# Issuing the first weight load of a decode kernel ahead of the opening barrier

## The chip, the cores and the metric

The kernel runs on one core of one Trainium2 chip. The metric is the device time of one execution in microseconds; each run also has the span, from the start of the program's first instruction to the end of its last. A load is issued by an instruction, its data then come in packets, and it lands when all have arrived.

## The reference

A decode step: the gated sum of an attention block over a cached K and V and of a small dense block.

```python
# x: 2 x 1 x 448, wq: 448 x 4096, k_cache, v_cache: 2 x 8 x 32768 x 256, wo: 4096 x 448, all bf16
g = sigmoid((x * gate_w).sum(-1, keepdims=True))
q = (x @ wq).reshape(B, 1, 16, 256).transpose(0, 2, 1, 3)
p = softmax(einsum("bhqd,bhkd->bhqk", q, repeat(k_cache)) * 256 ** -0.5)
a = einsum("bhqk,bhkd->bhqd", p, repeat(v_cache)).transpose(...).reshape(...) @ wo
b = gelu(x @ w1 + b1) @ w2 + b2           # w1: 448 x 1792, w2: 1792 x 448
out = g * a + (1 - g) * b
```

The two caches are 537 MB of the 547 MB that must be read. Everything else is small.

## The kernel before

SyncE issues all large loads, in one order: WQ (two parts), W1 (two parts), then K and V tiles of 8 MB in turn, and W2 and WO at the end. The tiles go round three slots of on-chip memory. A load is issued when the work that read its slot has ended. ScalarE's queue brings six small loads: x, the gate (two rows), the biases b1 and b2 (three loads).

```python
def prog_sp(E):
    def dma(fn, stream, key):
        E.ins(fn, key=key, stream=stream)

    for d in order:
        for pd in before_of[d]:
            E.wait("pe", released(pd))          # wait until the slot is free
        kind, idx = d
        if kind == "WQ":
            parts = [(wq_f, A_wq[0:KC * P, :].rearrange("(p k) n -> p (k n)", p=P), "d_wq0"),   # 3 MB
                     (wq_r, A_wq[KC * P:Dm, :].rearrange("p (h n) -> (p h) n", h=2), "d_wq1")]  # 0.5 MB
            for i, (o, src, _) in enumerate(parts):
                dma(lambda e, o=o, src=src: e.dma_start(o, src), "slot0", ("wq", i))
        elif kind == "W1":
            ...                                  # 1.3 MB and 0.2 MB
        ...
        else:
            src = kv_src(A_k_cache if kind == "K" else A_v_cache, idx)
            dma(lambda e, src=src, d=d: e.dma_start(cut(slot_of[d], 0, SLOT), src),
                f"slot{slot_of[d]}", ("fill", d))
    ...

def prog_act(E):
    dma(lambda e: e.dma_start(x_sb, A_x[:, 0, :]), "d_x", "x")
    ...                                          # gate, b1, b2: five more small loads
```

The programs of the five engines start in a block. Ahead of it the framework puts an opening block: GpSimd writes four constants, every engine drains and reports to GpSimd, and GpSimd releases them all. This is the opening barrier.

```python
with nc.Block("main") as block:
    def run(nm, eng):
        engs[nm].eng = eng
        progs[nm](engs[nm])

    block.gpsimd(lambda eng: run("pool", eng))
    block.sync(lambda eng: run("sp", eng))
    ...
```

Of the kernel before, what the change touches and what calls it, by code (L numbers as in the profile page):

```python
# [125 lines left out]
def bass_gated_mix__gqa_block_cached__dense_activation_gelu__decode_kernel(  # L126
# [27 lines left out]
    _, Hkv, Sk, Dh = A_k_cache.shape  # L154
# [4 lines left out]
    P = 128  # L159
# [11 lines left out]
    KC = 3  # L171
# [29 lines left out]
    with contextlib.ExitStack() as es:  # L201
# [65 lines left out]
        def kv_src(cache, idx):  # L267
            g, t = idx // NT, idx % NT
            b, kvh = grp(g)
            return cache[b, kvh, t * P * R:(t + 1) * P * R, :].rearrange("(p r) d -> p (r d)", p=P)  # L270
# [32 lines left out]
        def released(d):  # L303
            kind, idx = d
            return {"K": ("S", idx, NCK // 2 - 1), "V": ("PV", idx), "WQ": "QT", "W1": "HT"}[kind]

        cut = lambda s, lo, n: ring[:, s * SLOT + lo:s * SLOT + lo + n]
        wq_f, wq_r = cut(0, 0, KC * HD), cut(0, KC * HD, HW)
# [31 lines left out]
        def prog_pool(E):  # L340
# [13 lines left out]
            for b in range(Bn):  # L354
                E.ins(lambda e, b=b: e.affine_select(
                    out=tsel[:, 136 * b:136 * b + 136], in_=tsel[:, 136 * b:136 * b + 136], compare_op=ALU.not_equal,
                    fill=1.0, base=256 - 128 * b, pattern=[[-1, 136]], channel_multiplier=-8), key=f"ts{b}")

        def prog_sp(E):
            def dma(fn, stream, key):  # L360
                E.ins(fn, key=key, stream=stream)

            for d in order:
                for pd in before_of[d]:
                    E.wait("pe", released(pd))
                kind, idx = d
                if kind == "WQ":
                    parts = [(wq_f, A_wq[0:KC * P, :].rearrange("(p k) n -> p (k n)", p=P), "d_wq0"),
                             (wq_r, A_wq[KC * P:Dm, :].rearrange("p (h n) -> (p h) n", h=2), "d_wq1")]
                    for i, (o, src, _) in enumerate(parts):  # L370
                        dma(lambda e, o=o, src=src: e.dma_start(o, src), "slot0", ("wq", i))
                elif kind == "W1":
                    parts = [(w1_f, B_w1[0:KC * P, :].rearrange("(p k) n -> p (k n)", p=P)),
                             (w1_r, B_w1[KC * P:Dm, :].rearrange("p (h n) -> (p h) n", h=2))]
                    for i, (o, src) in enumerate(parts):
                        dma(lambda e, o=o, src=src: e.dma_start(o, src), "d_w1", ("w1", i))  # L376
                elif kind == "W2":
                    dma(lambda e: e.dma_start(w2_f, B_w2.rearrange("(p f) n -> p (f n)", p=P)), "d_w2", "w2")
                elif kind == "WO":
                    src = A_wo.rearrange("(p c) n -> p (c n)", p=P)  # L380
                    for i in range(len(WOP) - 1):
                        c0, c1 = WOP[i] * Dm, WOP[i + 1] * Dm
                        dma(lambda e, src=src, c0=c0, c1=c1: e.dma_start(wo_v[:, c0:c1], src[:, c0:c1]), f"pW{i}", ("wo", i))  # L383
                elif d == ("V", LASTV):
                    src, base, r0 = kv_src(A_v_cache, idx), slot_of[d] * SLOT, 0
                    for i, n in enumerate(PIECES):
                        c0, c1 = r0 * Dh, (r0 + n) * Dh
                        dma(lambda e, c0=c0, c1=c1: e.dma_start(ring[:, base + c0:base + c1], src[:, c0:c1]),
                            f"pV{i}", ("piece", i))
                        r0 += n  # L390
# [4 lines that stand above are left out]
            E.wait_total("mix")  # L395
            dma(lambda e: e.dma_start(out[:, 0, :], out_sb), "d_out", "out")
            E.wait_total("d_out")
# [260 lines left out]
        def prog_dve(E):  # L658
# [134 lines left out]
            E.ins(lambda e: e.tensor_copy(out_sb[:, 0:DQ], ps_a[0:Bn, :]), key="mixd", stream="mix")  # L793

        progs = {"pool": prog_pool, "sp": prog_sp, "pe": prog_pe, "act": prog_act, "dve": prog_dve}
        engs = {nm: _Eng(sch, nm) for nm in progs}
        sch.plan = True
        for nm, f in progs.items():
            f(engs[nm])
        for stream, key in sch.reqs:  # L800
            assert key in sch.streams[stream].events, f"missing event {stream}:{key}"
        sch.plan = False
        sch.reset_counts()
        with nc.Block("main") as block:
            def run(nm, eng):
                engs[nm].eng = eng
# [4 lines that stand above are left out]
            block.tensor(lambda eng: run("pe", eng))  # L811
            block.scalar(lambda eng: run("act", eng))
            block.vector(lambda eng: run("dve", eng))
# [28 lines left out]
```

## Time and profile before

| kernel before | |
|---|---|
| time, median of 6 runs | 1272.86 us (1272.69 to 1272.92) |
| span of the profiled run | 1270.7 us |
| bytes moved, mean rate | 547.61 MB, 431 GB/s |
| first WQ load issued | 0.74 us |
| first packets of the stream | 1.77 us |
| last WO piece that the end waits for landed | 1268.12 us |

The page of the kernel before, cut to the DMA. The second line is the busy share of the DMA engines in tenths, in 40 equal slices of the span; the queue line gives packets, MB and the share of 16 engines' span that their packets took.

```profile
span 1270.7 us, 8089 instructions
...
DMA  9999999999999999999999999999999999999998
...
DMA packets 11116, 547.61 MB, mean 431 GB/s; under 512 B 1368, under 2 KB 1632, under 8 KB 2144
...
q1 hardware_dynamic: 10948, 547.43, 99.7%
q8 instruction: 9, 0.15, 0.0%
```

The engines that move data are busy all the time. Two edges are left, and the first is visible in the timeline of the opening (start, duration, engine; "SPq" is SyncE's own queue of instructions):

```profile
0.24 0.10 POOL L827 MEMSET const-float32-0.0<- 128x1 f32 x1 [0.24 <-issue]
...
0.73 0.56 ACTq L602 DMA_DIRECT2D pexp<-in_A_x_dram  x1
0.73 0.20 POOL L341 MEMSET ident_b<- 128x128 bf16 x1 [0.29 <-POOLq L827]
0.74 0.88 SPq L371 DMA_DIRECT2D ring<-in_A_wq_dram  x2
...
1.67 1.11 SPq L376 DMA_DIRECT2D ring<-in_B_w_dram  x2
...
2.81 22.79 SPq L393 DMA_DIRECT2D ring<-in_A_k_cache_dram  x3
```

SyncE begins at 0.00 us, yet issues its first load at 0.74 us. The list of SyncE's waits names what it did in between; L827 is the barrier:

```profile
SPq L827 <- PEq L827: 0.7, 1, 0.7
```

When the data begin to move is shown by short windows of the same kernel. The last two columns are the DMA share and GB/s. A packet is counted whole in the window in which it starts, so the share can be above 1: only the first window with a large number matters.

```profile
core 0: us, PE busy (x) PEld busy (x) DVE busy (x) ACT busy (x) POOL busy (x), PEclk, DMA share, GB/s
1.60:1.75 0.15, 0.00 (x0) 0.00 (x0) 0.15 (x1) 0.00 (x0) 0.15 (x2) 1.00 0.06 12
1.75:1.90 0.15, 0.00 (x0) 0.00 (x0) 0.15 (x1) 0.00 (x0) 0.15 (x2) 1.00 5.54 1311
```

The stream starts in the second window (the records have the first packet at 1.77 us), 1.03 us after the start of the issue, or 0.62 us after its end, since the first issue takes 0.41 us. Two lines of the chain of waits (start, duration, what) give the landing of the first K tile and of the fourth of WO's five pieces: 2.81 + 33.52 = 36.33 us and 1227.23 + 40.88 = 1268.11 us. The fifth piece, 0.9 KB a row, lands at 1268.38 us, while the matmuls on the fourth still follow each other without a break. So the fourth is the last piece that the end waits for; it is what the prediction and the text below call the last WO piece.

```profile
2.81 33.52 DMA ring<-in_A_k_cache_dram
...
1227.23 40.88 DMA ring<-in_A_wo_dram
```

### The profile page before, as it was taken

How to read it: one execution, taken by the hardware profiler on the slowest of the kernel's cores; microseconds unless marked ns; L12 is line 12 of the kernel's file. 1: busy time of each engine (PE TensorE's matmuls, PEld its weight loads, DVE VectorE, ACT ScalarE, POOL GpSimd, SP SyncE). 2: the span in 40 equal slices, each digit the busy share in tenths (PEclk: the TensorE clock that was granted, in tenths of full speed). 3: DMA queues.
4: the chain of work that ended last, by engine and by line, in shares of the span. 5: the costliest groups of instructions: out<-in, count | busy, mean ns of one | idle time of the engine just before them, and what ended most of it. 6: DMA issues, size and time to landing. Idle time of an engine off the chain costs nothing.

```text
span 1270.7 us, 8089 instructions
## 1 busy us (share of the span) xinstructions
PE 701.6 (55%) x4544; PEld 146.4 (12%) x2016; DVE 685.8 (54%) x528; ACT 43.7 (3%) x183; POOL 3.3 (0%) x14
## 2 busy tenths in 40 slices
PE   4666556644476454665545665445664436655465
PEld 3111111100011100111100111000110001111012
DVE  2875536655365563556735466453665636556341
ACT  1000000000000000000000000000000000000000
POOL 1000000000000000000000000000000000000000
PEclk9987788767787767887777787678877778876787
DMA  9999999999999999999999999999999999999998
GB/s 405 444 430 435 428 432 433 434 431 438 431 431 429 441 433 433 435 431 433 429 435 437 433 433 435 431 431 429 441 433 433 431 435 431 431 435 437 433 422 371
DMA packets 11116, 547.61 MB, mean 431 GB/s; under 512 B 1368, under 2 KB 1632, under 8 KB 2144
## 3 DMA queue, kind: packets, MB, share of 16 engines
q1 hardware_dynamic: 10948, 547.43, 99.7%
q8 instruction: 9, 0.15, 0.0%
q10 hardware_dynamic: 156, 0.01, 0.0%
q14 instruction: 3, 0.02, 0.0%
HBM read 547.43 MB, written 0.00 MB: 431 GB/s over the span
## 4 chain that ended last, share of the span: by engine, by line
DMA 63%; DVE 19%; PE 15%; issue 3%; SPq 0%; another core or an unknown queue 0%
DMA ring<-in_A_k_cache_dram 59%; DVE ring L722 17%; PE ps_s L490 5%; PE ps_s L335 4%; PE ps_o L335 4%; DMA ring<-in_A_wo_dram 3%; DVE mx L726 1%; PE ps_o L539 1%; PE ps_m L504 0%; PE ps_m L499 0%; DVE gmax L728 0%; DVE gmx L732 0%; SPq L383 0%; SPq L376 0%
## 5 line engine op out<-in xcount | busy, mean ns | idle before, releaser
L722 DVE STREAM_TRANSPOSE ring<-ring 128x2048 uint32<-128x2048 uint32 x256 | 565.2, 2275 | 385.1 <-DMA ring<-in_A_k_cache_dram 384.8
L490 PE MATMUL ps_s<-ring,Abd 128*128 128x512 bf16 x1024 | 426.5, 416 | 424.1 <-DVE ring L722 423.7
L335 PE MATMUL ps_s<-ring,Abd 128*128 128x512 bf16 x1024 | 422.5, 413 | 0.0
L490 PEld LDWEIGHTS ps_s<-ring,Abd 128*128 128x128 bf16 x1024 | 106.1, 104 | 846.8 <-DVE ring L722 475.4
L335 PE MATMUL ps_o<-ring,PT 128*24 128x512 bf16 x1504 | 115.4, 415 | 0.0
L539 PE MATMUL ps_o<-ring,PT 128*24 128x512 bf16 x544 | 58.9, 432 | 14.0 <-DMA ring<-in_A_v_cache_dram 14.0
L509 PE MATMUL ps_f<-o_sb,selg 128*32 128x257 f32 x32 | 17.0, 634 | 83.5 <-DVE o_sb L763 83.5
L763 DVE SCALAR_TENSOR_TENSOR o_sb<-ps_o,mask,o_sb 128x256 f32<-128x256 f32 x112 | 54.1, 483 | 9.9 <-PE ps_o L539 6.0
L726 DVE TENSOR_REDUCE mx<-ps_s 128x1 f32<-128x1024 f32 x16 | 19.6, 1224 | 59.8 <-PE ps_s L335 59.8
L636 ACT ACTIVATE negm<-ps_m 128x1 f32<-128x1 f32 x16 | 2.7, 171 | 1155.9 <-PE ps_m L504 1155.9
L739 DVE STREAM_TRANSPOSE PT<-pexp 128x1024 bf16<-128x1024 bf16 x16 | 19.9, 1244 | 41.1 <-PE ps_o L335 41.1
L539 PEld LDWEIGHTS ps_o<-ring,PT 128*24 128x24 bf16 x544 | 14.8, 100 | 108.0 <-issue 89.3
L736 DVE COPY ls<-lsum 128x1 f32<-128x1 f32 x16 | 2.5, 154 | 32.3 <-ACT pexp L640 32.3
L630 ACT COPY Abd<-qrep 32x16 bf16 (+1 forms) x128 | 19.5, 199 | 0.6
L640 ACT ACTIVATE pexp<-ps_s,negm 128x1024 bf16<-128x1024 f32 x16 | 17.8, 1114 | 1.7
L499 PE MATMUL ps_m<-ident_f,mx 128*1 128x128 f32 x32 | 6.1, 271 | 21.1 <-DVE mx L726 21.1
L760 DVE TENSOR_SCALAR o_sb<-ps_o,mask 128x256 f32<-128x256 f32 x16 | 7.6, 474 | 16.7 <-PE ps_o L335 16.7
L509 PEld LDWEIGHTS ps_f<-o_sb,selg 128*32 128x32 f32 x32 | 2.9, 140 | 101.9 <-DVE o_sb L763 99.8
L504 PE MATMUL ps_m<-ones_f,gmx 1*128 1x1 f32 x32 | 6.5, 272 | 9.9 <-DVE gmx L732 9.9
L728 DVE TENSOR_REDUCE gmax<-ps_m 1x2 f32<-1x128 f32 x16 | 4.5, 278 | 7.5 <-PE ps_m L499 7.5
L420 PE MATMUL ps_s<-xT,ring 128*128 128x2 bf16 x128 | 3.6, 165 | 8.0 <-DMA ring<-in_A_wq_dram 8.0
L504 PEld LDWEIGHTS ps_m<-ones_f,gmx 1*128 1x128 f32 x32 | 5.2, 201 | 14.6 <-DVE gmx L732 14.6
(76 smaller groups left out, 63.9 us busy)
## 6 DMA issues: line engine op xcount, KB each, us to landing
ring<-in_A_v_cache_dram SPq DMA_DIRECT2D x1, 4096.0 KB, 27.0
ring<-in_A_v_cache_dram SPq DMA_DIRECT2D x2, 2048.0 KB, 33.7
ring<-in_A_wq_dram SPq DMA_DIRECT2D x1, 3072.0 KB, 10.3
ring<-in_B_w_dram SPq DMA_DIRECT2D x1, 1568.0 KB, 34.3
ring<-in_A_wo_dram SPq DMA_DIRECT2D x1, 1568.0 KB, 37.7
ring<-in_B_w_dram SPq DMA_DIRECT2D x1, 1344.0 KB, 13.6
ring<-in_A_wo_dram SPq DMA_DIRECT2D x1, 1008.0 KB, 39.7
ring<-in_A_wo_dram SPq DMA_DIRECT2D x1, 560.0 KB, 40.5
```

The source lines that it names most:

```text
L335: return e.add_instruction(mybir.InstMatmult(name=f"I-{nc.next_id()}", engine=mybir.EngineType.PE, ldweights=False, ins=[e.lower_ap(x), e. ...
L490: fn = lambda e, o=o, x=x, st=st, sp=sp, s=s, w=w: e.matmul(o, a_win(s, w), x, start=st, stop=sp, skip_group_check=True)
L504: E.ins(lambda e: e.matmul(ps_m[:, C_BC:C_BC + 1], gmx[:, :], ones_f[0:1, 0:1], start=True, stop=True), key=("M2", g))
L509: E.ins(lambda e: e.matmul(ps_oa, selg[:, :], o_sb[:, :], start=False, stop=False, skip_group_check=True), key=("OT", g))
L539: fn = lambda e, o=o, x=x, wt=wt, st=st, sp=sp, j=j: e.matmul(o, wt, x, start=st, stop=sp, skip_group_check=True)
L630: E.ins(lambda e, o=o, Q=Q, c=c: e.copy(o[:, :, c:c + 2], qrep[32 * Q:32 * Q + 32, :, bass.ds(E.dyn(2 * g, 2), 2)]), key=(("A", g) if (Q = ...
L640: E.ins(lambda e: e.activation(pexp[:, :].rearrange("p (r i a) -> p i r a", r=CR, i=2), ps_s[:, :].rearrange("p (i r a) -> p i r a", i=2, ...
L722: E.ins(lambda e: e.transpose(k_words(idx, blk), k_words(idx, blk)), key=("T", idx, blk))
L726: E.ins(lambda e: e.tensor_reduce(mx[:, :], ps_s[:, :], AX.X, ALU.max), key=("MX", g))
L739: E.ins(lambda e: e.transpose(PT[:, :], pexp[:, :]), key=("PT", g))
L760: E.ins(lambda e, p=p, m=m: e.tensor_scalar(o_sb[:, 0:Dh], p, m, None, op0=ALU.mult), key=("OS0", g))
L763: E.ins(lambda e, p=p, m=m: e.scalar_tensor_tensor(out=o_sb[:, 0:Dh], in0=p, scalar=m, in1=o_sb[:, 0:Dh], op0=ALU.mult, op1=ALU.add), key= ...
```

## The change

SyncE is to issue the first part of WQ before it takes part in the opening barrier. The load needs nothing from the other engines: its slot is empty and its semaphore is its own. The instruction is built like any other, and then moved ahead of SyncE's drain in the opening block.

```diff
+        def first_load(E):
+            src = A_wq[0:KC * P, :].rearrange("(p k) n -> p (k n)", p=P)
+            E.ins(lambda e: e.dma_start(wq_f, src), key=("wq", 0), stream="slot0")
+
         def prog_sp(E):
@@
-                    for i, (o, src, _) in enumerate(parts):
+                    for i, (o, src, _) in list(enumerate(parts))[1:]:
                         dma(lambda e, o=o, src=src: e.dma_start(o, src), "slot0", ("wq", i))
@@
         sch.plan = True
+        first_load(engs["sp"])
         for nm, f in progs.items():
             f(engs[nm])
@@
         sch.reset_counts()
+
+        entry = nc.main_func.blocks[-1]
+        n0 = len(entry.instructions)
+        engs["sp"].eng = nc.sync
+        first_load(engs["sp"])
+        ins = entry.instructions
+        at = next(i for i, x in enumerate(ins) if x.engine == mybir.EngineType.SP and type(x).__name__ == "InstDrain")
+        entry.instructions = ins[:at] + ins[n0:] + ins[at:n0]
         with nc.Block("main") as block:
```

## The prediction

> **What bounds the kernel.** The DMA stream. The page has DMA in the top tenth in all but the last slice, 547.61 MB at a mean of 431 GB/s, and 99.7% of 16 engines' span spent by the packets of SyncE's queue. The windows view gives a DMA share of 1.00 and 433 GB/s from 30 to 1200 us. The Trainium skill, "DMA: Bandwidth & Descriptors", section "Where 436 GB/s comes from", puts the ceiling of the 16 engines at 435.2 GB/s; this trace agrees. The DMA records show 16 packets in flight without a visible gap from 1.9 to 1266.3 us. Only two edges are left: no data until 1.77 us, and about 4.4 us after the packets thin out (last matmuls, two copies, the output store). PE (55%) and DVE (54%) are not the limit. SyncE's waits on PE (993.7 us in all) pass with one or two 8 MB loads still queued: a load lands 27 to 50 us after its issue and takes 19.35 us to move, so these waits do not empty the queue.
>
> **What changes.** SyncE's first instruction, at 0.00 us, is the drain of the opening barrier; the barrier releases it at 0.65 us (the waits view: 0.7 us) and the first WQ load (3 MB) is issued at 0.74 us. Its first packets start at 1.77 us, 1.03 us after the issue. After the change the issue is SyncE's first instruction, at 0.00 to 0.1 us; so first packets at 1.03 to 1.15 us, 0.6 to 0.74 us sooner.
>
> The issue takes 0.41 us, so SyncE comes to the barrier at about 0.45 us. GpSimd, which collects the arrivals, does so at 0.53 us, after its own constants and drain: I expect the barrier to end when it did, at most 0.1 us later. The second WQ load is then issued at about 0.74 us in place of 1.20, and SyncE's other opening issues about 0.46 us sooner. 3 MB is about 7 us of stream, so no gap opens between the two.
>
> **What lies on the critical path.** All of the shift: the stream has no slack from first packet to last, so every landing, every buffer release and the last WO piece (lands at 1268.12 us) come about 0.7 us sooner. The compute of the opening does not count: the first K load lands at 36.3 us, and PE and DVE are done with WQ and W1 at about 27 us. The small loads on ScalarE's queue now meet WQ packets already in flight and may land 1 to 2 us later (x now at 2.1 us, the last bias at 12.1 us); that is absorbed in the slack before 36 us.
>
> **Prediction: 1272.15 us** (0.7 us or 0.05% less), range 1271.7 to 1272.8. Faster by over 2%: 0.3%; within 2%: 99%; slower by over 2%: 0.7%.
>
> **What would show it right.** Span near 1270.0 us; the WQ issue first in SyncE's timeline; first data near 1.05 us; K's first landing near 35.6 us in place of 36.34; the last WO piece near 1267.4; DMA share still 1.00 in the middle; the same 2.6 us from the last WO landing to the end.
>
> **What would make it wrong.** (a) The drain behind the issue waits for the load's data: the barrier would end some 9 us late, the stream would run dry after WQ and the kernel be about 3 us slower. (b) The first issue takes longer, or its data start later, when nothing ran before it: gain nearer 0.3 us. (c) The stream's rate differs by 0.05% from run to run, which hides the gain. (d) Somewhere the stream is paced by buffer releases, not by its start: then the lead is lost at the first such wait.

## The result and the profile after

The changed kernel took 1272.23 us (median of 6 runs, 1272.08 to 1273.18) against 1272.86 us for the kernel before in the same rounds. Ratios in this document are the mean time of one kernel's runs over that of the other's of the same rounds, so they are not quite the ratio of the medians; here it is 0.9996, with an interval of 0.9983 to 1.0009. By that interval alone the two kernels can't be told apart. All runs together tell more: of 34 runs of the kernel before, the profiled one among them, the fastest took 1272.63 us, and 8 of 11 runs of the changed kernel (6 here, 5 in the first experiment) are below that. The spans separate the two kernels fully: the 28 recorded for the kernel before lie between 1270.7 and 1271.3 us (median 1270.9), the 11 of the changed kernel between 1270.0 and 1270.3 us (median 1270.2). The slow run here, 1273.18 us, has a span of 1270.1 us, no longer than its neighbours, so its extra 1 us lies outside the span.

The page, the timeline, the windows and the chain of the changed kernel, in the order in which those of before were shown:

```profile
span 1270.3 us, 8089 instructions
...
DMA  9999999999999999999999999999999999999998
...
DMA packets 11115, 547.59 MB, mean 431 GB/s; under 512 B 1368, under 2 KB 1632, under 8 KB 2144
```

```profile
0.00 0.41 SPq L361 DMA_DIRECT2D ring<-in_A_wq_dram  x1
0.23 0.10 POOL L840 MEMSET const-float32-0.0<- 128x1 f32 x1 [0.23 <-issue]
...
0.81 0.20 POOL L341 MEMSET ident_b<- 128x128 bf16 x1 [0.37 <-POOLq L840]
0.81 0.55 ACTq L606 DMA_DIRECT2D pexp<-in_A_x_dram  x1
0.81 0.33 SPq L375 DMA_DIRECT2D ring<-in_A_wq_dram  x1
...
2.25 22.89 SPq L397 DMA_DIRECT2D ring<-in_A_k_cache_dram  x3
```

```profile
0.80:1.00 0.20, 0.00 (x0) 0.00 (x0) 0.00 (x0) 0.00 (x0) 0.20 (x2) 1.00 0.00 0
1.00:1.20 0.20, 0.00 (x0) 0.00 (x0) 0.00 (x0) 0.00 (x0) 0.20 (x3) 1.00 3.15 737
```

```profile
2.25 33.24 DMA ring<-in_A_k_cache_dram
...
1228.37 39.30 DMA ring<-in_A_wo_dram
```

The issue stands first, and its data move from 1.03 us, again 1.03 us after the start of the issue. The other engines leave the barrier about 0.08 us later (GpSimd's first own instruction moves from 0.73 to 0.81 us). The first K tile lands at 35.49 us, 0.84 us sooner; the last WO piece at 1267.67 us, 0.44 us sooner. So the lead is there, but it is not one number. To follow it I used the trace's DMA records in two ways: the time at which the stream has moved a given number of bytes (each packet's bytes spread over its time), and the landings on each of the 16 engines, which report separately.

| | before | after | sooner by |
|---|---|---|---|
| first packet of the stream | 1.77 | 1.03 | 0.74 |
| mean start of the first sixteen packets | 1.95 | 1.30 | 0.64 |
| 1 MB moved | 5.02 | 4.39 | 0.63 |
| 100 MB moved | 234.19 | 233.58 | 0.62 |
| 545 MB moved | 1261.29 | 1260.70 | 0.59 |
| last WO piece, mean of 16 engines | 1267.25 | 1266.66 | 0.59 |
| last WO piece, slowest engine | 1268.12 | 1267.68 | 0.44 |
| end of the span | 1270.71 | 1270.26 | 0.45 |

The lead of the stream is set in the ramp (the first microseconds, in which the engines start one after another), and is almost unchanged 1260 us later. The engines do not start together: their first packets start over 0.8 to 1.0 us, and the mean of the sixteen moves by 0.64 us, not by 0.74. At the end the kernel waits for the slowest engine alone, and that one moved by 0.44 us in this pair of profiles. The pair flatters the kernel before: its profile, 1270.7 us, is at the short end of its spans, and that of the changed kernel, 1270.3 us, at the long end of its own.

### The profile page after: what moved, and what is told of

Read it like the earlier page. It is cut to its first block, busy times and chain, and to the rows that moved or that the text cites. A ratio compares the mean times of both kernels' runs of the same rounds, so it can differ in the third digit from the quotient of the medians.

```text
span 1270.3 us, 8089 instructions
## 1 busy us (share of the span) xinstructions
PE 707.1 (56%) x4544; PEld 147.2 (12%) x2016; DVE 685.8 (54%) x528; ACT 43.7 (3%) x183; POOL 3.3 (0%) x14
## 4 chain that ended last, share of the span: by engine, by line
DMA 59%; DVE 19%; PE 16%; issue 3%; another core or an unknown queue 2%; SPq 0%; ACT 0%; DVEq 0%
DMA ring<-in_A_k_cache_dram 56%; DVE ring L726 17%; PE ps_s L494 5%; PE ps_s L335 5%; PE ps_o L335 4%; DMA ring<-in_A_wo_dram 3%; DVE mx L730 1%; PE ps_o L543 1%; PE ps_m L508 0%; PE ps_m L503 0%; DVE gmax L732 0%; DVE gmx L736 0%; SPq L387 0%; ACT pexp L644 0%
## 5 line engine op out<-in xcount | busy, mean ns | idle before, releaser
L764 DVE TENSOR_SCALAR o_sb<-ps_o,mask 128x256 f32<-128x256 f32 x16 | 7.6, 474 | 16.1 <-PE ps_o L335 16.1
```

The lines of the kernel that those rows point to most:

```text
L764: E.ins(lambda e, p=p, m=m: e.tensor_scalar(o_sb[:, 0:Dh], p, m, None, op0=ALU.mult), key=("OS0", g))
```

## The experiments

Three theories stood against each other. The stream theory: the program is one DMA stream without slack, and its end moves as its start moves. The rival: what helped is that SyncE's other opening issues also came 0.39 to 0.56 us sooner. The third, the barrier theory: the time of the opening barrier and of the compute behind it counts. Two more are tested on the way: that the gain is noise, and the release theory, by which buffers that come free pace the stream somewhere on the way, so that a late start is caught up. Every time is set against the kernel before in the same rounds. "Lead" is that of the stream at 545 MB, against the one profile of the kernel before shown above.

| run | median us | kernel before | difference | lead in the stream | WO landing, mean and slowest engine | span |
|---|---|---|---|---|---|---|
| changed kernel | 1272.23 | 1272.86 | -0.63 | 0.59 | 1266.66, 1267.68 | 1270.3 |
| e1_again | 1272.15 | 1272.97 | -0.82 | 0.67 | 1266.58, 1267.44 | 1270.0 |
| e2_hold | 1276.11 | 1272.97 | +3.14 | -3.25 | 1270.49, 1271.73 | 1274.3 |
| e3_rest_late | 1272.16 | 1272.97 | -0.81 | 0.67 | 1266.58, 1267.53 | 1270.1 |
| e4_four_ahead | 1272.33 | 1272.97 | -0.64 | 0.73 | 1266.52, 1267.83 | 1270.4 |
| e5_small_first | 1273.02 | 1272.85 | +0.17 | 0.46 | 1266.78, 1268.25 | 1270.8 |
| e6_small_loads_late | 1292.11 | 1272.85 | +19.26 | -19.02 | 1286.27, 1287.31 | 1289.9 |
| e7_dry | 1274.44 | 1272.85 | +1.59 | -1.77 | 1269.02, 1270.11 | 1272.7 |
| e8_unrolled | 1276.01 | 1272.85 | +3.16 | -1.07 | 1268.30, 1271.69 | 1274.3 |
| e9_small_then_large_ahead | 1272.48 | 1273.13 | -0.65 | 0.70 | 1266.54, 1267.91 | 1270.5 |
| e10_small_loads_4us | 1272.30 | 1273.13 | -0.83 | 0.64 | 1266.61, 1267.98 | 1270.6 |

In every row the span ends 2.58 to 2.59 us after the slowest engine's landing of WO: the tail does not change, and the whole of the differences between these spans lies in the stream. The slowest engine lands 0.86 to 1.47 us behind the mean in the kernels with loops, and this lag blurs the last two columns.

**e1_again.** The changed kernel unchanged.

> The changed kernel unchanged, for the noise. The stream theory (the end moves by as much as the first data of the DMA stream move, less what is lost in the ramp): 0.6 us under the kernel before, span 1270.1 to 1270.3. The noise theory (the 0.6 us seen was scatter between sessions): within 0.2 us of the kernel before.

It took 1272.15 us (1271.97 to 1272.69) against 1272.97 us. Its five spans, 1270.0 to 1270.3 us, lie below all nine of the kernel before in the same rounds, 1270.7 to 1271.3 us. The noise theory falls. The stream's lead was 0.67 us this time: two profiles of one program differ by 0.08 us.

**e2_hold.** The kernel before, with SyncE held.

```diff
 def prog_sp(E):
     ...
+    E.wait("pool", "ts1")
     for d in order:
```

> The kernel before, with SyncE's whole program held until GpSimd's last setup instruction (about 4.05 us), so that the first load is issued about 3.35 us later than 0.74 us. Stream theory: the end is later by the same 3.35 us, about 1276.2 us. Release theory (somewhere on the way the stream is paced by buffers coming free or by PE and DVE, which absorb a late start): clearly less than 3 us later.

SyncE's timeline up to the first K loads:

```profile
4.05 0.88 SPq L372 DMA_DIRECT2D ring<-in_A_wq_dram  x2
...
6.20 22.55 SPq L394 DMA_DIRECT2D ring<-in_A_k_cache_dram  x3
```

The first issue moved by 3.31 us, the stream at 545 MB by 3.25 us, the time by 3.14 us. Nothing in the 1260 us that follow took a late start up. The release theory falls: in this kernel a microsecond at the start is a microsecond at the end.

**e3_rest_late.** The changed kernel, with all but the first load held; the diff is that of e2_hold, on the changed kernel.

> The changed kernel, with only the first WQ load early; all of SyncE's later issues are held until about 4.1 us (second WQ load 0.81 to about 4.2 us, first K load 2.25 to about 5.7 us). Stream theory: the 3 MB of the first load feed the engines until about 8 us, so the time is that of the changed kernel, 1272.2 us within 0.15. Rival (the gain comes from SyncE's other opening issues, which came 0.39 to 0.56 us sooner): these are now 3.4 us later, so about 1275.6 us.

```profile
0.00 0.41 SPq L361 DMA_DIRECT2D ring<-in_A_wq_dram  x1
4.10 0.33 SPq L376 DMA_DIRECT2D ring<-in_A_wq_dram  x1
4.47 0.92 SPq L381 DMA_DIRECT2D ring<-in_B_w_dram  x2
5.43 19.34 SPq L398 DMA_DIRECT2D ring<-in_A_k_cache_dram  x3
```

1272.16 us, in all 5 runs 1272.39 us or less. The later issues came 3 us later than in either kernel, and it cost nothing. The rival falls: the gain is that of the one load in front, as long as its 3 MB keep the engines busy until the next.

**e4_four_ahead.** All four weight loads in front of the barrier.

```diff
 def first_load(E):
     ...
+    rest = [(wq_r, ..., "slot0", ("wq", 1)), (w1_f, ..., "d_w1", ("w1", 0)), (w1_r, ..., "d_w1", ("w1", 1))]
+    for o, src, stream, key in rest:
+        E.ins(lambda e, o=o, src=src: e.dma_start(o, src), key=key, stream=stream)
@@
-                if kind == "WQ":
+                if kind in ("WQ", "W1"):
+                    continue
+                if kind == "WQ":
```

> The changed kernel with all four weight loads ahead of the opening barrier, not the first alone. SyncE comes to the barrier at about 2 us in place of 0.58, so every other engine starts about 1.4 us later. Stream theory: first data at 1.03 us as before, so the time is that of the changed kernel, 1272.2 us within 0.15; x and the gate land later and the slack before the first K load takes it. Barrier theory (what counts is when the engines start): about 1.4 us slower than the changed kernel, 1273.6 us.

```profile
0.00 0.41 SPq L361 DMA_DIRECT2D ring<-in_A_wq_dram  x1
0.46 0.41 SPq L366 DMA_DIRECT2D ring<-in_A_wq_dram  x1
0.92 1.14 SPq L366 DMA_DIRECT2D ring<-in_B_w_dram  x2
2.47 22.54 SPq L404 DMA_DIRECT2D ring<-in_A_k_cache_dram  x3
```

1272.33 us (1272.24 to 1272.46). The barrier let the engines go at about 2.4 us instead of 0.73, and the time is that of the changed kernel. The barrier theory falls. SyncE's drain took 0.12 us behind the four issues, as behind the one, against 0.01 us in the kernel before; it never waited for the data. More than the first load in front brings nothing.

**e5_small_first.** The small part of WQ in front, the large one behind the barrier.

```diff
-            src = A_wq[0:KC * P, :].rearrange("(p k) n -> p (k n)", p=P)
-            E.ins(lambda e: e.dma_start(wq_f, src), key=("wq", 0), stream="slot0")
+            src = A_wq[KC * P:Dm, :].rearrange("p (h n) -> (p h) n", h=2)
+            E.ins(lambda e: e.dma_start(wq_r, src), key=("wq", 0), stream="slot0")
```

> The changed kernel, with the small part of WQ (0.5 MB, 4 KB rows) ahead of the barrier and the large part (3 MB) behind it, issued at about 0.81 us. Stream theory: what counts is when the first data move, and 0.5 MB (1.2 us of stream plus a ramp of about 1 us) lasts until the large part's first packets at about 1.85 us: 1272.2 us, within 0.2 of the changed kernel. Rival (it takes the large load to gain, since it covers the later issues): most of the gain is lost, 1272.7 us or more.

A miss: 1273.02 us (1272.50 to 1274.25), nothing gained. The data began at 1.02 us and the lead was 0.84 us at 1 MB, more than in the changed kernel, but 0.41 us at 10 MB. The records show 14.2 stream packets in flight between 3 and 4 us, where the changed kernel has 16.1: some engines had run out of the small load. That alone is not the whole miss: at 545 MB the stream still led by 0.46 us, but in this profile the slowest engine landed 1.47 us behind the mean, against 0.87 us in the kernel before, and that took the whole of it. The spans of the five runs (median 1270.9 us, as in the kernel before) show no gain either.

**e9_small_then_large_ahead.** Both parts of WQ in front, small one first, made to find where e5's lead went.

```diff
-            E.ins(lambda e: e.dma_start(wq_f, src), key=("wq", 0), stream="slot0")
+            E.ins(lambda e: e.dma_start(wq_r, small), key=("wq", 0), stream="slot0")
+            E.ins(lambda e: e.dma_start(wq_f, src), key=("wq", 1), stream="slot0")
```

> Both WQ loads ahead of the barrier, the small one first and the large one right behind it, issued at about 0.46 us in place of 0.81. e5 with the small load first and the large one behind the barrier kept a lead of only 0.41 us of the 0.75 us by which its first data were early. If that loss is a gap between the two loads (engines that ran out of the small load before the large one reached them), it goes: the lead in the stream is back near 0.65 us and the time is 1272.2 us. If it comes of the order (packets of the large load that start behind the small ones move more slowly, as the 401 to 407 GB/s between 4 and 12 us in e5 against 420 to 431 in the changed kernel suggest), it stays: 1272.7 to 1273.0 us.

The lead at 545 MB is back at 0.70 us, with 16.05 packets in flight between 3 and 4 us; the time is 1272.48 us, 0.65 us under the kernel before. So closing the gap between the two loads wins back 0.24 us of stream against e5. The packets missing in e5 between 3 and 4 us are worth (16.1 - 14.2) / 16, about 0.12 us, an estimate, so the gap is a part of what e5 lost. The fall of e5's lead between 1 and 10 MB is mostly something else: e9, without the gap, fell from 1.00 to 0.63 us, nearly as much as e5 from 0.84 to 0.41 us. The windows from 4 to 12 us of e5, the changed kernel and e9, in this order, show the slower stream of both:

```profile
4.00:12.00 8.00, 0.27 (x5) 0.21 (x5) 2.17 (x8) 0.76 (x3) 0.07 (x1) 1.00 0.92 375
4.00:12.00 8.00, 0.27 (x5) 0.22 (x5) 1.83 (x7) 0.82 (x3) 0.07 (x1) 1.00 0.97 411
4.00:12.00 8.00, 0.67 (x20) 0.65 (x21) 1.73 (x7) 1.01 (x2) 0.54 (x2) 1.00 0.94 388
```

The stream ran at 410 to 416 GB/s from 4 to 8 us in e9, against 430 in the changed kernel, so the order costs something too, and the slowest engine ended 1.4 us behind the mean (1.0 us in the changed kernel). Why, these runs do not tell.

**e6_small_loads_late.** ScalarE's small loads held until WQ has landed.

```diff
 def prog_act(E):
+    E.wait("slot0", ("wq", 1))
     dma(lambda e: e.dma_start(x_sb, A_x[:, 0, :]), "d_x", "x")
```

> The changed kernel, with ScalarE's six small loads (x, gate, biases) held until WQ has landed at about 12 us in place of 0.81 us. It tests the slack of the opening compute: x then lands near 18 us in place of 7.0, the Q product and the dense layer follow some 10 us later. Stream theory: the engines have 16 us and more of queued loads at that time, so 1272.2 us, within 0.2 of the changed kernel. Rival (the opening compute is close to the critical path, so that the later landing of x costs part of the gain): several us slower.

The largest miss: 1292.11 us. Three views of this kernel, the timeline, SyncE's waits and a window, show the way from a small load to a dry stream:

```profile
12.91 0.60 ACTq L613 DMA_DIRECT2D PT<-in_B_b_dram  x2
...
53.90 0.38 DVE L696 CAST gp_sb<-PT 2x448 f32<-2x448 bf16 x1 [22.38 <-DMA PT<-in_B_b_dram]
```

```profile
SPq L100 <- PE ps_m L447: 58.1, 1, 58.1
```

```profile
53.00:62.00 9.00, 7.44 (x74) 6.41 (x74) 1.07 (x7) 0.00 (x0) 0.00 (x0) 1.00 0.01 2
```

The bias, 0.9 KB a row, was issued at 12.9 us and used at 53.9 us. VectorE's copy of it stands in front of the values that the dense layer's product waits for, so the product ended late, WQ's slot came free after 58 us of waiting (21.5 us in the changed kernel), and the third K tile could not be issued before the first two were through: from 53 to 62 us the engines moved 2 GB/s. The Trainium skill, "DMA: Bandwidth & Descriptors", section "Queues, rings and completion order", says that each DMA engine takes turns between the queues at packet granularity. This trace fits that: the packets that the biases shared the engines with were of 64 KB, about 2.4 us each, and every small packet waits its turn behind one: in the records the last of ScalarE's small packets start at 40.9, 43.3, 45.7, 48.2, 50.6 and 53.0 us, one about every 2.4 us. So "the compute of the opening does not count" holds within a slack, and the slack can be used up by loads of a few bytes.

**e10_small_loads_4us.** The same hold, but until GpSimd's last setup instruction.

```diff
 def prog_act(E):
+    E.wait("pool", "ts1")
     dma(lambda e: e.dma_start(x_sb, A_x[:, 0, :]), "d_x", "x")
```

> The changed kernel, with ScalarE's small loads held until about 4.1 us in place of 0.81 (e6 held them until 11.4 us and lost 19 us, since the last bias was then caught between 64 KB packets of the K loads and landed at 53 us). If only that is what cost e6 its time, these loads still pass mostly among WQ's 24 KB packets, the last bias lands before about 20 us, and the time is that of the changed kernel, 1272.2 us within 0.2. If the opening compute has hardly any slack, each us of delay costs about a us: 1275 us.

1272.30 us. 3.3 us later cost nothing: the loads still passed among the packets of WQ and W1 (24 KB at most), and the last bias landed at 13.9 us, before the first 64 KB packet of K started at 14.05 us. The loss of e6 is thus that of falling among the K packets, not a microsecond for a microsecond.

**e7_dry.** SyncE's later issues held until the first load has landed, as if the drain waited for the data.

```diff
 def prog_sp(E):
     ...
+    E.wait("slot0", ("wq", 0))
     for d in order:
```

> The changed kernel, with SyncE's later issues held until the first WQ load has landed, as if the drain had waited for its data. Stream theory: the first load lands near 9 us, its last packets end near 8.5 us, and the next data come 1 us after the next issue, so the stream is dry for about 1.5 to 2.5 us: 1273.7 to 1274.7 us. Release theory (a late stream is caught up later): 1272.2 us.

The windows of the stretch, with the DMA share and GB/s at the end of each line:

```profile
8.00:9.00 1.00, 0.00 (x0) 0.00 (x0) 0.00 (x0) 0.00 (x0) 0.00 (x0) 1.00 0.93 394
9.00:10.00 1.00, 0.00 (x0) 0.00 (x0) 0.20 (x1) 0.00 (x0) 0.00 (x0) 1.00 0.06 5
10.00:11.00 1.00, 0.00 (x0) 0.00 (x0) 0.97 (x2) 0.00 (x0) 0.00 (x0) 1.00 0.00 0
11.00:12.00 1.00, 0.00 (x0) 0.00 (x0) 0.63 (x6) 0.20 (x1) 0.00 (x0) 1.00 0.68 193
```

In the records no stream packet runs from 9.9 to 11.2 us, an engine stands idle for about 2.1 us in the mean, and the stream is still at 392 GB/s from 12 to 13 us, against 429 in the changed kernel. The kernel took 1274.44 us, 1.59 us more than the kernel before; the lead in the stream went from +0.74 us at 1 MB to -1.77 us, a loss of 2.5 us. This hole was paid in full at the end. The release theory falls here too.

**e8_unrolled.** The changed kernel with its main loops unrolled, to test what spreads the 16 engines' landings.

```diff
-        with self.eng.Fori(0, n) as it:
-            self.at = (it, iter(self.vals))
-            body(0)
-            ...
-        st.count += (n - 1) * steps.pop()
+        for i in range(n):
+            body(i)
```

(Waits for events before the first iteration, which the loop form padded, are left out.)

> The changed kernel with its main loops unrolled on every engine, so that some 25 to 30 instruction fetches of 16 KB run beside the stream in place of 8. In the two profiles each fetch put one of the 16 DMA engines back by about 1.9 us (the mean landing of the 16 moves by about 0.12 us at each). If so, the mean engine ends about 2 to 2.5 us later, the last engine 2 us later or more, according to how the fetches spread: 1274.2 us at the least. If fetches are not what spreads the engines' landings: 1272.2 us and the same spread of 2.3 us at the end.

The page's line of instruction fetches, here and above for the kernel before, shows the dose (packets, MB):

```profile
q8 instruction: 26, 0.43, 0.1%
```

25 fetches of 16 KB ended before the last WO landing in place of 8 (the ninth on the page above came at 1268.5 us, after it), and the kernel took 1276.01 us. Against e1_again the mean landing of WO came 1.72 us later (2 to 2.5 us had been expected) and the slowest engine's 4.25 us; the first engine's landing moved by 0.3 us, the other way. So a fetch holds back the engine on which it runs: 1.72 us x 16 engines / 17 more fetches is about 1.6 us each, an estimate (four more packets of 8 KB on another queue of instruction fetches are left out of it). The kernel before shows the same size without e8's other changes: between 35 and 1200 us the mean landing of an 8 MB tile follows that of the tile before by 19.351 us in the 55 steps with no fetch, and by 19.453 us in the four with one fetch of 16 KB; 0.10 us in the mean of 16 engines is 1.6 us on one. The Trainium skill, "Runtime: NRT & Kernel Launch", section "Instruction fetch mechanics", has the cost of crossing a 16 KiB boundary as mostly hidden. It speaks of the engine that runs the instructions; the stream that fills every DMA engine pays, as these landings show. The unrolled loops also lose their branches, and a loop's wait values differ, so that part of the 4 us may have other causes; that the stream of one group of engines falls back while the first keeps its time is what the landings show.

In the looped kernels the 8 fetches are part of every run. Between 10 us and the end the gap between the first and the slowest engine's landing grows from 1.1 to 2.2 us in the kernel before, and from 1.3 to 2.3 us in the changed one, in steps at the fetches. The slowest landing differs from run to run (1267.44 and 1267.68 us in the two profiles of the changed kernel); that the fetches hit other engines each time is a guess, since the records do not name the engine. Together with the scatter outside the span (1.9 to 3.1 us of it in the runs of the changed kernel) this is the likely reason why 0.6 us of lead shows as 0.45 us in one pair of profiles and as 0.8 us in one pair of medians; the share of each was not measured.

No kernel tried here is faster than the changed kernel beyond this scatter.

## Why the prediction was right

Point by point:

- **The bound: right.** The DMA share and the rate are the same after the change, and every hole or delay put into the stream was paid (e2_hold: 3.31 us at the issue, 3.14 us in the time; e7_dry: 2.1 us of idle engines and a slow ramp, a loss of 2.5 us in the stream).
- **The start of the stream: right.** First packets were predicted at 1.03 to 1.15 us and came at 1.03 us; the 1.03 us from the start of the issue to the data did not change with the place of the issue.
- **The barrier: right.** It ended 0.08 us later, "at most 0.1 us" had been said. SyncE came to it later than thought, at about 0.58 us and not 0.45, since the drain behind the issue took 0.12 us.
- **"All of the shift" reaches the end: right in kind, a little too large in size.** The five programs that issue the 3 MB load first and lose nothing later (the changed kernel, e1, e3, e4 and e10) kept 0.59 to 0.73 us of the 0.74 us by which their first packet came sooner, all against one profile of the kernel before. The mis-sized term is the shift, which the prediction took from the first packet. Where the difference goes is not shown: the mean start of the first sixteen packets moved by 0.64 us in the changed kernel, near its lead of 0.59 us, but by 0.75 us in e10 (lead 0.64 us) and by 0.61 us in e4 (lead 0.73 us). The last WO piece came at 1267.68 us in place of 1267.4, and the span was 1270.3 us in place of 1270.0, since the end waits for the slowest engine, whose lag is not the same in each run; the repeat had 1267.44 and 1270.0 us. "Every landing about 0.7 us sooner" was wrong as a statement on single landings: the first K landing came 0.84 us and the last WO landing 0.44 us sooner, as read on the slowest engine (0.62 and 0.59 us in the mean of the sixteen).
- **The small loads: wrong in size.** "1 to 2 us later" was 4.9 us for x (2.1 to 7.0 us), 1.7 us for the gate and 0.8 us for the last bias. That it is absorbed was right (e4_four_ahead and e10_small_loads_4us delay them further at no cost), but the reason given, slack until 36 us, was too simple: e6_small_loads_late shows that loads held until 11.4 us fall among packets almost three times as large (64 KB and 24 KB) and then cost 19 us.
- **What could have made it wrong.** The drain did not wait for the data (0.12 us). What it would have cost if it had is not shown: e7_dry, made in its likeness for SyncE alone, ended 1.59 us over the kernel before, but there the other engines and the small loads were not late, which cost 19 us in e6_small_loads_late. Risks (b) and (d) did not come true either. Risk (c) did in part: the spans of the kernel before scatter over 0.6 us, about 0.05%, and the interval of the single comparison includes no difference at all.
- **The time: right.** 1272.23 us against 1272.15, in the range; the two medians of the change are -0.63 and -0.82 us, around the -0.7 that was predicted. That they lie so close around it is partly luck, since the medians of the kernel before alone range from 1272.85 to 1273.13 us; but the median spans, free of the scatter outside, also differ by 0.7 us.

## What to carry to other kernels

When a kernel is one DMA stream from its first packet to its last, as this one is, look first at the time of its first issue: here one load large enough to cover the next issues, put before anything the queue would wait for, took the whole gain, and more loads in front brought nothing. Make sure that it does cover them: the small load in front gained nothing here, in part since the engines ran out of it. And look at where the small loads go when the big ones move forward, because here a few bytes between large packets arrived some 40 us after their issue.

## What the Trainium skill lacked or had wrong

- "DMA: Bandwidth & Descriptors", section "Latency and other measured facts", has about 600 ns to the first byte for loads issued from SyncE or ScalarE. It does not say from when they count. The first packet started 0.62 us after the end of the first issue, which agrees, but 1.03 us after its start, since the issue itself took 0.41 us; both were the same behind the barrier and as the program's first instruction. The page also lacks that the first sixteen packets are spread over another 0.8 to 1.0 us in the two kernels.
- No page that I read says whether a drain behind a DMA issue waits for the load's data. Here it does not: it took 0.12 us, in front of data that landed 10 us later, and 0.01 us with no issue before it; behind four issues it was 0.12 us again.
- No page that I read has the cost of a program's own opening barrier. SyncE was released from it 0.65 us after its first instruction, and 2.4 us after it when it arrived at 2.2 us.
- "Runtime: NRT & Kernel Launch", section "Instruction fetch mechanics", calls the crossing of a 16 KiB boundary mostly hidden and has nothing on its cost to a DMA stream. Beside this saturated stream each 16 KB fetch held one DMA engine back by about 1.6 us (estimate from 17 more fetches and 1.72 us in the mean landing, and again from 0.10 us in the mean landing of the tiles with a fetch in the kernel before).
- "DMA: Bandwidth & Descriptors", section "Queues, rings and completion order", has the turn-taking between queues but no size of the wait. Here it was about 2.4 us for each small packet: a bias of 0.9 KB a row issued at 12.9 us was used at 53.9 us among 64 KB packets.
